# Another order for the hand-over from the expert layer to the last layer of an attention, soft-MoE and SoLU kernel

## The chip, the core and the metric

The kernel runs on one NeuronCore of a Trainium2 chip. The metric is the time of one launch in device microseconds (us), taken as the median of repeated runs. The core has five engines that work through queues of their own: TensorE (PE in the profile; its weight loads are PEld), VectorE (DVE), ScalarE (ACT), GpSimd (POOL) and SyncE (SP, which issues DMAs). An engine runs its instructions strictly in the order in which the program gives them, and waits on semaphores where it needs what another engine makes. So one waiting instruction also holds up what stands behind it on its engine.

## The reference

Three layers follow each other. The last one reads what the middle one writes for all 3072 tokens.

```python
def _attn_ref(q, k, v, mem_k, mem_v):            # 4 batches, 8 heads, 768 tokens, 64 wide, chunks of 32
    ...                                          # softmax(q k / 8) v over a window and 8 memory keys
def _moe_ref(x, phi, w1, w2):                    # x: 3072 x 512, 8 experts of 4 slots, F = 1024
    logits = x @ phi
    d = np.exp(logits - logits.max(0, keepdims=True))
    d /= d.sum(0, keepdims=True) + 1e-09
    slot_input = (d.T @ x).reshape(E, S_per_e, D)
    for e in range(E):
        slot_out[e] = np.maximum(slot_input[e] @ w1[e], 0.0) @ w2[e]
    c = np.exp(logits - logits.max(1, keepdims=True))
    c /= c.sum(1, keepdims=True) + 1e-09
    return c @ slot_out                          # 3072 x 512
def _moe2_ref(x, w_in, w_out, g_ln):
    h = x @ w_in                                 # 3072 x 1024
    e = np.exp(h - np.max(h, axis=-1, keepdims=True))
    solu = h * (e / (np.sum(e, axis=-1, keepdims=True) + 1e-09))
    mu = np.mean(solu, axis=-1, keepdims=True)
    var = np.mean((solu - mu) ** 2, axis=-1, keepdims=True)
    return ((solu - mu) / np.sqrt(var + 1e-06) * g_ln) @ w_out
```

## The kernel before

**Stages.** Until about 115 us the kernel does attention and the dispatch sums of the experts; until 168.8 us the experts' matmuls, while their weights still come in; then a hand-over of some 20 us; then the last layer over 24 tiles of 128 tokens, to the end. The change touches the hand-over and the first tiles of the last layer.

**The hand-over.** Since `h = (c @ slot_out) @ w_in = c @ M` with `M = slot_out @ w_in`, the kernel makes M once (32 rows, 1024 columns) and then each tile's `h` (128 x 1024, two PSUM banks) from M and that tile's `c`. `slot_out` lies in bank 4 as four partial sums. `m_so` (L556) copies it to SBUF in two halves, both on ACT, and sums and turns it on PE (L562); DVE copies the result (L563). `m_in` (L566) multiplies by `w_in` in four parts (L569), which ACT copies out (L573, L574) as `mps`. Tile 0 takes its `h` straight from `mps` in plain fp32, in two halves (`emit_h(0)`, L662). The other tiles wait for M in a rounded form: `m_sum` (L581) sums M on PE, one half into the PSUM bank that later takes tile 0's output and one half into tile 1's `h`; `m_top` (L584, ACT) rounds it, `m_low` (L588, DVE) takes what was rounded off. Their `h` is then two fast matmuls (L662 again, from `m4`). `keep_clock` (L550) issues matmuls whose results nobody reads.

**A tile of the last layer.** DVE takes the maximum of `h` (`emit_max`, L668); ACT the exponential `e` and its sum (`emit_e`, L671); DVE the product `u` of both and its sum (`emit_u`, L677), which ends the use of `h`; `emit_y` (L689 to L697) takes the mean off and rearranges. There are two buffers of `h` (`h0`, `h1`), so tile n+2's `h` may not be written before tile n's `u` is done. For tiles 0 to 3 PE turns `y` (eight transposes, L719), ACT rounds the result (`emit_hi`, L740) and DVE takes the rest (`emit_lo`, L744); for tiles 4 to 23 the turn goes through DRAM and a DVE transpose (L733). Then come 24 matmuls of 128x512 (`emit_main`, L750): eight of hi by the rounded weights `whi`, eight of hi by their low parts `wlo`, eight of lo by `whi`. ACT scales the output by `rstd` (L768), which GpSimd works out (L704 to L716). `sq` (L700) is ACT's sum for the variance.

**The last weights.** `whi` and `wlo` of `w_out`'s last eighth (`wh7`) are made during the hand-over: seven steps of `wout_ops` (L632), each an `l` in `TAIL`: ACT L604 and L605, DVE L608 to L622, ACT L639 for `whi`, DVE L643 for `wlo`. PE needs them for the last matmuls of tile 0.

**What sets the order.** The engines' order is the order of the calls. In the hand-over it is the list `TAIL` (L57). From there on `final` (L778) gives each step of each tile a due time and calls them in the order of these times: `begin` (when a tile's matmuls should start) and `front` (when its front part should) come from a few numbers and the table `FRONT` (L52) for the first tiles, `HS` (L53) holds the times of the first tiles' `h`, and `OFF` (L55) holds the offsets of a tile's steps. The times only sort; what an engine really waits for is a semaphore.

Of the kernel before, what the change touches and what calls it, by code (L numbers as in the profile page):

```python
# [7 lines left out]
FP32 = mybir.dt.float32  # L8
# [25 lines left out]
FC = FF // P  # L34
# [14 lines left out]
NCONST = 425  # L49
NPE, NZ = 4, 4  # L50
T0, TPE, TDM, TF, LEAD, TT, TO, TH = 6.2, 6.85, 5.51, 3.0, 16.3, 3.8, 6.3, 2.2
FRONT = (0.0, 5.5, 8.1, 15.5, 15.1)  # L52
HS = (0.0, 1.2999999999999998, 4.8, 10.3, 12.9)  # L53
YON = 'daddp'
OFF = {'max': 0.25, 'e': 1.7, 'u': 3.3, 'y': 3.6, 'sq': 5.25, 'var': 5.75, 'rstd': 10.0, 'yt': -2.6, 'hi': -2.1, 'lo': -0.1, 'st': 3.65, 'fe': 7.75, 'tr': 0.0, 'hi2': 0.45, 'lo2': 3.95, 'mh': 0.68, 'ml0': 3.4, 'ml': 0.21, 'l0': 0.7, 'l1': 7.25}  # L55

TAIL = (  # L57
    "so open l l l min l l e12 ha hb max s0 s1 t0 e keep w0 u t1 y0 y1 l w1 yt0 hi0 yt1 hi1 lo0 l lo1 e3"
).split()

SPR = ("pp", "ap")
# [3 lines left out]
CLATE = 3  # L65
TORD = [1, 0]
TKEEP = [2, 1]
KEEP = (0, 2, 0, 10)

KS = GREC * REC  # L70
KT = GREC * CH
# [7 lines left out]
def tile_kernel(ctx: ExitStack, tc: tile.TileContext, kr, vr, w1, w2, w_in, w_out, cst, out):  # L79
# [45 lines left out]
    def bank(i):  # L125
        return banks[i]
# [428 lines left out]

    def m_so():  # L556
        for half in range(2):
            act.copy(out=so_sb[:, 256 * half:256 * half + 256], in_=bank(4)[:, 256 * half:256 * half + 256])
        bk = bank(2)
        keep_clock(bank(5), KEEP[1])  # L560
        for k in range(KC):
            pe.matmul(out=bk[:, k * 32:(k + 1) * 32], lhsT=so_sb[:, k * 128:(k + 1) * 128], rhs=i4, start=True, stop=True)  # L562
        dve.tensor_copy(out=sot, in_=bk[:, 0:128].rearrange("p (k s) -> p k s", k=KC))  # L563
        keep_clock(bank(5), KEEP[2])

# [13 lines left out]
    def m_sum(half):  # L579
        sl = slice(512 * half, 512 * half + 512)  # L580
        pe.matmul(out=m_of(half), lhsT=i4rep, rhs=mps[:, sl], start=True, stop=True)  # L581
# [50 lines left out]
    def wout_ops(j, t):  # L632

        w = wo[t % len(wo)]

        def hi():
            area(f"w{j}", [(f"wh{j}", DM), (f"wl{j}", DM)])
            whi[j], wlo[j] = at(f"wh{j}", 0, DM, FP32R), at(f"wl{j}", 0, DM, FP32R)
            act.activation(out=whi[j], in_=w, func=ACTF.Copy, scale=g_sb[:, j:j + 1])  # L639

        return cast_ops(slot_of["wout", j], at("tmp", 512 * (t % 2), 512), w, dve) + [
            hi,
            lambda: dve.scalar_tensor_tensor(  # L643
                out=wlo[j], in0=w, scalar=g_sb[:, j:j + 1], in1=whi[j].bitcast(FP32), op0=ALU.mult, op1=ALU.subtract
            ),
        ]


    def tps(i, sl):
# [2 lines left out]
        return fin["t"][:, sl]  # L652

    def sc(name, i):
        k = ("nm", "s", "nu", "vs", "x", "t", "r").index(name)
        o = 64 + 16 * (i % 8) + k
        return small[:, o:o + 1]

# [7 lines left out]

    def emit_max(i):
        dve.tensor_reduce(out=sc("nm", i), in_=fin["h"][i % 2], axis=AX.X, op=ALU.max, negate=True)  # L668

    def emit_e(i):  # L670
        act.activation(  # L671
# [106 lines left out]
    def final():  # L778

        steps = []  # L780

        def put(t, f, *args):
            steps.append((t, len(steps), f, args))

        begin = [T0]
        for n in range(NTILE):
            begin.append(begin[-1] + (TPE if n + 1 < NPE else TDM))
        front = list(FRONT)
        for n in range(len(front), NTILE):
            front.append(max(front[-1] + TF, begin[n] - LEAD))  # L790
        for n in range(NTILE):
            a, b = front[n], begin[n]
            w = OFF
            if n >= 1:
                put(HS[n] if n < len(HS) else a - TH, emit_h, n)
                put(a + w["max"], emit_max, n)
                put(a + w["e"], emit_e, n)
                put(a + w["u"], emit_u, n)
                put(a + w["y"], emit_y, n)
            put(a + w["sq"], emit_sq, n)  # L800
            put(a + w["var"], emit_var, n)
            put(a + w["rstd"], emit_rstd, n)
            if 1 <= n < NPE:
                for f in range(FC):
                    put(b + w["yt"], emit_yt, n, f)
                put(b + w["hi"], emit_hi, n)
                put(b + w["lo"], emit_lo, n)
            if n >= NPE:
                put(a + w["st"], emit_store, n)
                put(a + w["fe"], emit_fetch, n)  # L810
                put(b - TT + w["tr"], emit_turned, n)
                put(b - TT + w["hi2"], emit_hi, n)
                put(b - TT + w["lo2"], emit_lo, n)
            if n == NTILE - 1:
                put(b + w["l0"], emit_last, n, 0)
                put(b + w["l1"], emit_last, n, 1)
                continue
            for f in range(FC):
                put(b + w["mh"] * f, main_hi, n, f)
                put(b + w["ml0"] + w["ml"] * f, main_lo, n, f)  # L820
            put(b + TO, emit_out, n)
        for t, _, f, args in sorted(steps, key=lambda x: x[:2]):
            f(*args)

    with tc.manual_schedule():
# [176 lines left out]
        for x in TAIL[:first]:  # L1002
# [3 lines left out]
        ob = [at("ob", 512 * i, 512) for i in range(3)]  # L1006
        sq = at("sq", 0, 1024)
        calls.update(
            h0=lambda: emit_h(0), ha=lambda: emit_h(0, (0,)), hb=lambda: emit_h(0, (1,)), max=lambda: emit_max(0), s0=lambda: m_sum(0), s1=lambda: m_sum(1),
            keep=lambda: keep_clock(fin["o"][1], KEEP[3]), t0=lambda: m_top(0), t1=lambda: m_top(1),  # L1010
            w0=lambda: m_low(0), w1=lambda: m_low(1), e=lambda: emit_e(0), u=lambda: emit_u(0),
            y0=lambda: emit_y(0, 0), y1=lambda: emit_y(0, 1),
# [74 lines left out]
```

## Time and profile before

| | |
|---|---|
| median of 3 runs | 330.57 us (330.4 to 331.27) |
| the profiled execution | 330.6 us, of which 328.8 us from its first to its last instruction |
| PE busy | 298.1 us (91%) |
| DVE, ACT, POOL busy | 237.7, 222.3, 168.0 us |
| end of the experts' matmuls | 168.8 us |
| first of tile 0's 24 matmuls | 180.83 us |
| tile 0's last matmul ends | 188.96 us |

Times in the profile are us from the first instruction. An engine's busy time does not tell what holds the kernel up; for this the chain of waits is read, which follows the end of the kernel back to what released each step, and the timeline of an engine, in which the idle time before an instruction and its releaser stand in brackets.

### The profile page before, as it was taken

The page shows a single profiled execution, that of the slowest core. Times are in us where ns is not written, and L with a number is a line of the kernel's source. Part 1 is how long each engine was busy: PE and PEld are TensorE (multiplying, and loading weights), DVE is VectorE, ACT ScalarE, POOL GpSimd, SP SyncE. Part 2 cuts the span into 40 slices and gives each one's busy share as a digit, 9 for nine tenths or more (in the row PEclk, how much of TensorE's full clock was granted, in tenths as well). Part 3 has the DMA queues.
Part 4 walks back from the last instruction along what each step waited for, and adds up shares of the span by engine and source line. Part 5 has one row for each costly group of instructions (what it writes and reads, how often), then busy time and mean ns, then how long its engine had stood idle before and what let it go on. Part 6 is the DMA issues. An engine that isn't in the chain of part 4 may idle for free.

```text
span 328.8 us, 8291 instructions
## 1 busy us (share of the span) xinstructions
PE 298.1 (91%) x3069; PEld 217.1 (66%) x3069; DVE 237.7 (72%) x431; ACT 222.3 (68%) x441; POOL 168.0 (51%) x395
## 2 busy tenths in 40 slices
PE   2788898899797789888999999999999999999996
PEld 2576666777675433323335788888888888888885
DVE  6676887798778439999127986878878878787540
ACT  3566745866774537685536689998888888888721
POOL 5256577676675023233100557777676576676700
PEclk9999999999999999999999999999999999999999
DMA  7999999999999999999930005675756666566521
GB/s 290 420 380 400 418 413 418 416 412 401 415 421 420 419 425 426 424 425 421 421 141 0 1 35 218 232 251 205 244 219 204 252 207 223 220 235 234 194 96 65
DMA packets 32696, 95.85 MB, mean 291 GB/s; under 512 B 3856, under 2 KB 14480, under 8 KB 28944
## 3 DMA queue, kind: packets, MB, share of 16 engines
q1 hardware_dynamic: 32512, 95.11, 74.1%
q8 instruction: 24, 0.39, 0.5%
q10 hardware_dynamic: 144, 0.22, 0.2%
q14 instruction: 16, 0.13, 0.1%
HBM read 78.53 MB, written 16.78 MB: 290 GB/s over the span
## 4 chain that ended last, share of the span: by engine, by line
PE 63%; DMA 17%; DVE 10%; issue 3%; POOL 3%; ACT 2%; SPq 1%; POOLq 0%; ACTq 0%; DVEq 0%
PE bank L750 37%; DMA kq_area<-in_kr_dram 8%; PE bank L281 5%; DMA ex_area<-in_w_dram 5%; PE bank L337 4%; DMA e_area<-in_w_dram 4%; PE h L662 4%; POOL kq_area L330 3%; PE bank L319 2%; PE bank L360 1%; PE bank L407 1%; PE bank L348 1%; PE bank L524 1%; PE bank L760 1%; PE t L760 1%
## 5 line engine op out<-in xcount | busy, mean ns | idle before, releaser
L750 PE MATMUL bank<-wh_area,yh_area 128*128 128x512 f32 x552 | 129.8, 390 | 0.0
L750 PEld LDWEIGHTS bank<-wh_area,yh_area 128*128 128x128 f32 x552 | 103.4, 188 | 21.8
L330 POOL TENSOR_SCALAR kq_area<-kq_area 64x416 f32<-64x416 f32 x88 | 38.4, 441 | 36.5 <-DMA kq_area<-in_kr_dram 17.6
L281 PE MATMUL bank<-kq_area 128*32 128x128 f32 x768 | 29.7, 290 | 15.2 <-POOL kq_area L330 8.2
L733 DVE STREAM_TRANSPOSE yq_area<-yq_area 128x1024 f32<-128x1024 f32 x20 | 24.9, 1245 | 18.7 <-DMA yq_area<-z 18.7
L322 ACT COPY s_area<-bank 128x384 f32<-128x384 f32 x32 | 15.3, 478 | 33.3 <-PE bank L319 31.7
L677 DVE SCALAR_TENSOR_TENSOR eb_area<-h,eb_area 128x1024 f32<-128x1024 f32 x24 | 29.1, 1216 | 8.3 <-ACT eb_area L671 7.9
L281 PEld LDWEIGHTS bank<-kq_area 128*32 128x32 f32 x768 | 20.7, 115 | 21.5 <-POOL kq_area L330 12.1
L299 DVE TENSOR_REDUCE cst_area<-bank 128x6 f32<-128x384 f32 x32 | 17.7, 554 | 18.3 <-PE bank L281 18.0
L337 PE MATMUL bank<-vz_area,s_area 128*32 128x130 f32 x768 | 28.4, 275 | 2.7 <-DVE cst_area L299 1.2
L668 DVE TENSOR_REDUCE cst_area<-h 128x1 f32<-128x1024 f32 x24 | 29.0, 1216 | 0.9 <-PE h L662 0.9
L715 POOL TENSOR_SCALAR cst_area<-cst_area 128x1 f32<-128x1 f32 x72 | 25.4, 353 | 7.6
L671 ACT ACTIVATE eb_area<-h,cst_area 128x1024 f32<-128x1024 f32 x24 | 26.7, 1111 | 1.9 <-DVE cst_area L668 1.9
L700 ACT ACTIVATE eb_area<-eb_area,cst_area 128x1024 f32<-128x1024 f32 x24 | 27.3, 1138 | 0.1
L697 ACT ACTIVATE eb_area<-eb_area,cst_area 128x1024 f32<-128x1024 f32 x20 | 23.1, 1154 | 4.6 <-DVE eb_area L677 4.1
L744 DVE TENSOR_TENSOR yh_area<-yq_area,yh_area 128x1024 fp32r<-128x1024 f32 x20 | 24.5, 1226 | 2.3 <-ACT yh_area L740 2.3
L704 POOL TENSOR_SCALAR cst_area<-cst_area 128x1 f32<-128x1 f32 x24 | 15.6, 648 | 20.6 <-ACT eb_area L671 18.7
L740 ACT CAST yh_area<-yq_area 128x1024 fp32r<-128x1024 f32 x20 | 21.0, 1050 | 6.8 <-DVE yq_area L733 6.7
L716 POOL TENSOR_SCALAR cst_area<-cst_area 128x1 f32<-128x1 f32 x72 | 22.0, 305 | 7.1
L337 PEld LDWEIGHTS bank<-vz_area,s_area 128*32 128x32 f32 x768 | 21.7, 109 | 5.1 <-ACT s_area L355 1.4
L768 ACT ACTIVATE eb_area<-bank,cst_area 128x512 f32<-128x512 f32 x23 | 15.8, 686 | 8.5 <-POOL cst_area L706 5.5
L314 ACT ACTIVATE s_area<-s_area 128x384 f32<-128x384 f32 x32 | 17.0, 530 | 3.3 <-DVE s_area L305 3.2
(154 smaller groups left out, 526.5 us busy)
## 6 DMA issues: line engine op xcount, KB each, us to landing
e_area<-in_w_dram SPq DMA_DIRECT2D x15, 1024.0 KB, 9.9
kq_area<-in_kr_dram SPq DMA_DIRECT2D x32, 400.0 KB, 7.5
vz_area<-in_vr_dram SPq DMA_DIRECT2D x32, 390.0 KB, 6.8
ex_area<-in_w_dram SPq DMA_DIRECT2D x10, 1024.0 KB, 13.4
z<-eb_area SPq DMA_DIRECT2D x20, 512.0 KB, 2.7
yq_area<-z SPq DMA_DIRECT2D x80, 128.0 KB, 2.9
out_dram<-eb_area SPq DMA_DIRECT2D x23, 256.0 KB, 2.0
e_area<-in_w_in_dram SPq DMA_DIRECT2D x4, 1024.0 KB, 9.4
```

What stands on the lines that cost most here:

```text
L281: pe.matmul(out=bk[32 * j:32 * j + 32, t * 128:(t + 1) * 128], lhsT=kq[i][:, KT + c * CH:KT + (c + 1) * CH], rhs=kwin(g % 2, c), start=Tru ...
L330: pool.tensor_scalar(out=o, in0=i, scalar1=1.0, scalar2=0.0, op0=ALU.mult, op1=ALU.add)
L337: pe.matmul(out=bk[32 * j:32 * j + 32, t * 2 * VW:(t + 1) * 2 * VW], lhsT=atb[g % 2][:, c * CH:(c + 1) * CH], rhs=vz[g // 2 % 2][:, :, g % ...
L668: dve.tensor_reduce(out=sc("nm", i), in_=fin["h"][i % 2], axis=AX.X, op=ALU.max, negate=True)
L671: act.activation(out=eb[i % FIN], in_=fin["h"][i % 2], func=ACTF.Exp, bias=sc("nm", i), accum_out=sc("s", i))
L677: dve.scalar_tensor_tensor(out=ub[i % FIN], in0=fin["h"][i % 2], scalar=-1.0 / FF, in1=eb[i % FIN], op0=ALU.mult, op1=ALU.mult, accum_out= ...
L697: act.activation(out=yb[i % FIN], in_=ub[i % FIN], func=ACTF.Identity, scale=-float(FF), bias=sc("nu", i))
L700: act.activation(out=sq, in_=ub[i % FIN], func=ACTF.Square, scale=-float(FF), bias=sc("nu", i), accum_out=sc("vs", i))
L715: pool.tensor_scalar(out=t, in0=r, scalar1=r, scalar2=xx, op0=ALU.mult, op1=ALU.mult)
L733: dve.transpose(out=yv[i % FIN].rearrange("p (f a t) -> p a f t", f=FC, a=4), in_=yq[i % FIN].rearrange("p (a f t) -> p a f t", f=FC, a=4),)
L744: dve.tensor_tensor(out=yl[i % FIN][:, sl], in0=tps(i, sl) if i < NPE else yv[i % FIN], in1=yh[i % FIN][:, sl].bitcast(FP32), op=ALU.subtract,
L750: pe.matmul(out=fin["o"][i % 2], lhsT=a[i % FIN][:, f * 128:(f + 1) * 128], rhs=w[f], start=start, stop=stop)
```

## The change

It has six parts, all between 168.8 us and the first four tiles. (1) The second half of the slots' sum is copied by DVE instead of ACT. (2) Tile 0's maximum is taken by halves: each half of `h` is followed by its own reduction, and a small DVE instruction joins the two. (3) On ACT tile 0's exponential comes ahead of the two roundings of M, and on DVE `u` and the first half of `y` ahead of the two low parts of M. (4) The `h` of tiles 1 to 3 and their maxima move: tile 1's `h` and maximum stand in `TAIL` behind tile 0's first two main matmuls, tile 2's `h` two matmuls later, and the fronts of tiles 2 and 3 and the `h` of tiles 4 and 5 get later due times. (5) The low part of the last weights goes to GpSimd in two instructions. (6) Eight instead of ten `keep_clock` matmuls stand in the hand-over.

```diff
-FRONT = (0.0, 5.5, 8.1, 15.5, 15.1)
-HS = (0.0, 1.2999999999999998, 4.8, 10.3, 12.9)
+FRONT = (0.0, 5.5, 9.7, 16.6, 15.1, 22.0)
+HS = (0.0, 0.0, 6.9, 10.3, 15.0, 21.9)
...
-    "so open l l l min l l e12 ha hb max s0 s1 t0 e keep w0 u t1 y0 y1 l w1 yt0 hi0 yt1 hi1 lo0 l lo1 e3"
+    "so open l l l min l l e12 ha ma hb mb l l s0 s1 e t0 keep u t1 y0 y1 w0 w1 yt0 hi0 yt1 hi1 lo0 f0 h1 x1 lo1 e3"
...
-KEEP = (0, 2, 0, 10)
+KEEP = (0, 2, 0, 8)
...
-            act.copy(out=so_sb[:, 256 * half:256 * half + 256], in_=bank(4)[:, 256 * half:256 * half + 256])
+            move("ad"[half], so_sb[:, 256 * half:256 * half + 256], bank(4)[:, 256 * half:256 * half + 256])
...
-            lambda: dve.scalar_tensor_tensor(
+            lambda: low(w, j) if j == FC - 1 else dve.scalar_tensor_tensor(
                 out=wlo[j], in0=w, scalar=g_sb[:, j:j + 1], in1=whi[j].bitcast(FP32), op0=ALU.mult, op1=ALU.subtract
             ),
         ]
+
+    def low(w, j):
+        pool.tensor_scalar(out=w, in0=w, scalar1=g_sb[:, j:j + 1], scalar2=0.0, op0=ALU.mult, op1=ALU.add)
+        pool.tensor_tensor(out=wlo[j], in0=w, in1=whi[j].bitcast(FP32), op=ALU.subtract)
...
+    def max_half(half):
+        dve.tensor_reduce(
+            out=sc("nm1" if half else "nm", 0), in_=fin["h"][0][:, part(half)], axis=AX.X, op=ALU.max, negate=True
+        )
+        if half:
+            dve.tensor_tensor(out=sc("nm", 0), in0=sc("nm", 0), in1=sc("nm1", 0), op=ALU.min)
...
-            if n >= 1:
+            if n >= 2:
                 put(HS[n] if n < len(HS) else a - TH, emit_h, n)
                 put(a + w["max"], emit_max, n)
+            if n >= 1:
                 put(a + w["e"], emit_e, n)
...
-                put(b + w["mh"] * f, main_hi, n, f)
+                if n or f:
+                    put(b + w["mh"] * f, main_hi, n, f)
```

In the changed file the lines stand lower: L662 became L666, L671 L682, L677 L688, L700 L711, L719 L730, L740 L751, L750 L761, L768 L779; L675 and L679 are `max_half`, L649 and L650 `low`. `Activation`, `DVE` and `Pool` are the semaphores of these engines.

**TensorE around tile 0's `h`.** `h_2249` is `h0`, `h_2250` is `h1`, `bank_84` and `bank_85` are the two output banks. Before:

```order
L569 MATMUL bank_85<-cst_area 32x512 x4
L662 MATMUL h_2249<-hr_area 128x512 [waits Activation_49] x2
L581 MATMUL bank_84<-hr_area,cst_area 128x512
L581 MATMUL h_2250<-hr_area,cst_area 128x512
L550 MATMUL bank_85<-wh_area,c4t_area 128x512 x10
```

Now:

```order
L569 MATMUL bank_85<-cst_area 32x512 x4
L666 MATMUL h_2249<-hr_area 128x512 [waits Activation_49]
L666 MATMUL h_2249<-hr_area 128x512 [waits DVE_49,Activation_49]
L581 MATMUL bank_84<-hr_area,cst_area 128x512
L581 MATMUL h_2250<-hr_area,cst_area 128x512
L550 MATMUL bank_85<-wh_area,c4t_area 128x512 x8
```

The second half of `h0` now also waits for DVE: for the first half's reduction (L675), the last DVE instruction that the program puts ahead of it.

**TensorE from tile 0's transposed `y` of the next tile to tile 1's matmuls.** `t` is the bank pair of the transposes. Before:

```order
L719 MATMUL t<-cst_area,eb_area 128x128 x7
L750 MATMUL bank_84<-wh_area,yh_area 128x512 x5
L662 MATMUL h_2249<-m_area,c4t_area 128x512 [waits DVE_49]
L662 MATMUL h_2249<-m_area,c4t_area 128x512
L750 MATMUL bank_85<-wh_area,yh_area 128x512 [waits Activation_49]
L750 MATMUL bank_85<-wh_area,yh_area 128x512 x9
```

Now:

```order
L730 MATMUL t<-cst_area,eb_area 128x128 x7
L761 MATMUL bank_84<-wh_area,yh_area 128x512 x3
L761 MATMUL bank_84<-wh_area,yh_area 128x512 [waits Pool_49]
L761 MATMUL bank_84<-wh_area,yh_area 128x512
L761 MATMUL bank_85<-wh_area,yh_area 128x512 [waits Activation_49]
L761 MATMUL bank_85<-wh_area,yh_area 128x512 x5
L666 MATMUL h_2249<-m_area,c4t_area 128x512 [waits DVE_49]
L666 MATMUL h_2249<-m_area,c4t_area 128x512
L761 MATMUL bank_85<-wh_area,yh_area 128x512 x13
```

Tile 4's `h` (in `h0`) moved from ahead of tile 1's matmuls to behind the sixth of them; the same pattern stands one tile later with tile 5's `h` in `h1`. From tile 6's `h` on, both orders are alike.

**ScalarE from tile 1's exponential on.** Before:

```order
L671 ACTIVATE eb_area,cst_area<-h_2250,cst_area 128x1024 [waits DVE_49]
L671 ACTIVATE eb_area,cst_area<-h_2249,cst_area 128x1024 [waits DVE_49,Activation_49]
L700 ACTIVATE eb_area,cst_area<-eb_area,cst_area 128x1024 [waits DVE_49]
L740 CAST yh_area<-t 128x1024 [waits PE_49]
L768 ACTIVATE eb_area<-bank_84,cst_area 128x512 [waits PE_49,Pool_49]
```

Now:

```order
L682 ACTIVATE eb_area,cst_area<-h_2250,cst_area 128x1024 [waits DVE_49]
L711 ACTIVATE eb_area,cst_area<-eb_area,cst_area 128x1024 [waits DVE_49]
L751 CAST yh_area<-t 128x1024 [waits PE_49]
L682 ACTIVATE eb_area,cst_area<-h_2249,cst_area 128x1024 [waits DVE_49]
L779 ACTIVATE eb_area<-bank_84,cst_area 128x512 [waits PE_49,Pool_49]
```

Tile 2's exponential (from `h_2249`) moved from right behind tile 1's to behind tile 1's rounding (the CAST), which waits for PE's transposes.

## Rows read from the trace of the kernel before

**Rows 1.** The page, busy time by engine and the granted clock in 40 slices

```profile
PE 298.1 (91%) x3069; PEld 217.1 (66%) x3069; DVE 237.7 (72%) x431; ACT 222.3 (68%) x441; POOL 168.0 (51%) x395
...
PEclk9999999999999999999999999999999999999999
```

**Rows 2.** Stretches: length, busy PE, PEld, DVE, ACT, POOL, clock, DMA share, GB/s

```profile
86.80:88.40 1.60, 0.13 (x5) 0.07 (x8) 1.31 (x4) 1.60 (x7) 1.39 (x4) 1.00 0.98 395
187.50:325.70 138.20, 138.15 (x640) 115.04 (x638) 101.98 (x109) 109.59 (x154) 86.27 (x252) 1.00 0.56 197
```

**Rows 3.** Chain of waits through the hand-over: start, us, what

```profile
172.62 1.93 PE h L662 x4
...
175.91 1.22 ACT eb_area L671 x2
...
177.16 1.25 DVE eb_area L677 x2
...
184.63 1.24 DVE eb_area L677 x2
...
188.96 0.46 PE h L662 x2
```

**Rows 4.** Timeline of ACT and PE, 168.5 to 172.6: start, us, idle before

```profile
168.81 0.65 ACT L558 COPY cst_area<-bank 128x256 f32<-128x256 f32 x2 [2.95 <-PE bank L542]
...
169.26 1.05 PE L562 MATMUL bank<-cst_area 128*128 128x32 f32 x8
```

**Rows 5.** Groups: count, then busy us and mean ns of one

```profile
L299 DVE TENSOR_REDUCE cst_area<-bank 128x6 f32<-128x384 f32 x32 | 17.7, 554 | 18.3 <-PE bank L281 18.0
...
L330 POOL TENSOR_SCALAR kq_area<-kq_area 64x416 f32<-64x416 f32 x44 | 25.0, 568 | 34.6 <-DMA kq_area<-in_kr_dram 17.6 <-PE bank L337 6.5 <-ACT kq_area L326 5.0
...
L622 POOL TENSOR_TENSOR cst_area<-cst_area 128x512 f32<-128x512 f32 x8 | 10.4, 1302 | 0.7
...
L693 POOL TENSOR_SCALAR eb_area<-eb_area,cst_area 128x1024 f32<-128x1024 f32 x1 | 1.1, 1127 | 0.1
...
L413 DVE COPY cst_area<-bank 96x512 f32<-96x512 f32 x1 | 0.7, 687 | 0.3 <-PE bank L407 0.3
...
L563 DVE COPY cst_area<-bank 128x128 f32<-128x128 f32 x1 | 0.3, 291 | 4.7 <-PE bank L562 4.7
```

**Rows 6.** Timeline of DVE

```profile
172.99 0.69 DVE L622 TENSOR_TENSOR wo_area<-wo_area,cst_area 128x512 f32<-128x512 f32 x1
174.57 1.22 DVE L668 TENSOR_REDUCE cst_area<-h 128x1 f32<-128x1024 f32 x1 [0.89 <-PE h L662]
...
178.83 0.74 DVE L588 SCALAR_TENSOR_TENSOR m_area<-cst_area,h 128x512 fp32r<-128x512 f32 x1
...
182.15 2.35 DVE L668 TENSOR_REDUCE cst_area<-h 128x1 f32<-128x1024 f32 x2
...
186.57 1.22 DVE L677 SCALAR_TENSOR_TENSOR eb_area<-h,eb_area 128x1024 f32<-128x1024 f32 x1
...
188.89 1.23 DVE L744 TENSOR_TENSOR yh_area<-t,yh_area 128x1024 fp32r<-128x1024 f32 x1 [0.30 <-ACT yh_area L740]
```

**Rows 7.** Timeline of DVE and POOL around 97.5: a small SBUF instruction beside GpSimd

```profile
97.28 1.29 POOL L622 TENSOR_TENSOR cst_area<-cst_area 128x512 f32<-128x512 f32 x1
...
97.57 1.02 DVE L375 TENSOR_TENSOR cst_area<-cst_area 96x1 f32<-96x1 f32 x1
```

**Rows 8.** Timeline of ACT

```profile
179.05 0.71 ACT L639 ACTIVATE wh_area<-wo_area,cst_area 128x512 fp32r<-128x512 f32 x1
179.67 0.58 ACT L740 CAST yh_area<-bank 128x512 fp32r<-128x512 f32 x1
...
187.84 1.02 ACT L740 CAST yh_area<-t 128x1024 fp32r<-128x1024 f32 x1 [0.70 <-PE t L719]
```

**Rows 9.** Timeline of PE

```profile
180.83 4.29 PE L750 MATMUL bank<-wh_area,yh_area 128*128 128x512 f32 x18
185.92 0.73 PE L662 MATMUL h<-m_area,c4t_area 128*128 128x512 f32 x2 [0.81 <-DVE eb_area L677]
```

## What the change is predicted to do

> **What bounds the kernel now.** I read the page first: TensorE is busy for 298.1 of 328.8 us, no other engine for more than 237.7, and the granted clock is in the top tenth of all 40 slices [rows 1]. Then the stretches. From 187.5 us to the end PE works 138.15 of 138.20 us, at clock 1.00 [rows 2], and its 640 matmuls take 138.15 / 640 = 0.216 us each. So nothing behind 187.5 has any room: a stall that is put into this part costs its full length, and one taken out before it is worth what tile 0's last matmul, which ends at 188.96 [rows 3], moves forward. The chain of waits shows what sets that time: from 172.62 on PE makes tile 0's `h`, then ACT its exponential, DVE `u`, and, some steps later, tile 1's `u`, whose end at 184.63 + 1.24 = 185.87 lets PE start tile 3's `h` [rows 3, 9]. The reader is to see there that PE has no work for 0.81 us before 185.92 [rows 9]. These 0.81 us, and the hand-over ahead of 180.83, are all that the change could win.
>
> **The change part by part.** Times are us in the profiled execution; sizes that the trace lacks are worked out from the nearest rows.
>
> *Copies of the slots' sum.* On ACT the two take 0.65 together, from 168.81 to 169.46 [rows 4]. In the changed order DVE's copy waits for ACT's. For 256 columns from PSUM DVE should need 0.42, between 0.291 for 128 and 0.687 for 512 [rows 5]: about 168.81 + 0.40 + 0.42 = 169.63. PE asks for the second half after half of its eight products, 169.26 + 0.52 = 169.78 [rows 4]. Gain 0; bounds +0.2 (a 0.6 us copy) and -0.1. The Trainium skill, page "PSUM — Partial Sum Buffer", section "PSUM bank collisions raise a hardware error", says that two engines at one bank's same partitions must be kept apart; both copies read bank 4, so by it too two engines give no overlap, and the sum would be the same. No row here shows such a pair.
>
> *Maximum by halves.* DVE's last piece of the weights ends at 172.99 + 0.69 = 173.68 [rows 6], so the first half's reduction runs 173.70 to 174.39: 0.69 is my value for 512 columns, between 0.554 for 384 [rows 5] and 1.22 for 1024 [rows 6]. TensorE's second half now waits for this reduction: the order shows DVE's semaphore at that matmul. It is issued at 174.4 and takes half of 1.93 [rows 3] and a restart of 0.1: 175.4. The second reduction ends at 176.1, the small joining instruction at 176.3 (0.16 for one column: the copies' 0.291 for 128 and 0.687 for 512 [rows 5] grow by 1.03 ns a column), and the exponential starts at 176.4, where it started at 175.91 [rows 3]: +0.5. So halves that should overlap follow each other. Behind PE's wait stand M's two sums, which nobody needs early.
>
> *Low part on GpSimd.* ACT's rounding takes 0.71 [rows 8] and now comes as soon as DVE's piece is ready at 173.68: to 174.4. GpSimd's scaling of 512 columns I put at 0.65 (568 ns for 416, 1127 for 1024), its subtraction at 1.30 [rows 5]: to 176.4. TensorE needs the result in its last matmuls of tile 0, near 188.4: hidden by 12 us, so its cost is nothing unless it disturbs a neighbour. One row shows such a disturbance: a DVE instruction on 96 numbers in SBUF took 1.02 us beside GpSimd's subtraction and ended with it, at 98.59 against 98.57 [rows 7]. The joining instruction at 176.1 is of that kind; it would end with GpSimd, near 176.5, and the exponential start at 176.6: +0.7. The Trainium skill, page "SBUF — State Buffer", section "SBUF: two separate sides", says why: the two engines share a port that one holds for a whole instruction. Without this lock the sum would be 0.2 less; the row agrees with the page. Taking the 0.74 us low part off DVE gains nothing itself, since tile 1's maximum, which stood behind it, will wait for `h`.
>
> *Exponential ahead of M's rounding; later `h`.* Tile 0's first rounding of `y` started at 179.67 and took 0.58 [rows 8]; it moves with the exponential and ends at 180.75 to 180.95. PE's first main matmul follows at 180.9 to 181.1, against 180.83 [rows 9]: four matmuls of `h` stood ahead of it and now come later, which wins back most of the delay. But tile 1's `h` now stands behind two main matmuls and lands some 1.15 later than these begin, at 182.05 to 182.25; before, its maximum started at 182.15 [rows 6], held by DVE. From there exponential and `u` take what they took. **Term A**: -0.05 to +0.2, taken as 0.1. The 0.81 idle is filled by matmuls that stood elsewhere; they are not saved.
>
> *First main matmul of tiles 1 and 2.* Before, the 0.46 pair of tile 4's `h` ran between tile 0's end (188.96 [rows 3]) and tile 1's first main matmul, which covered ACT's rounding, 187.84 + 1.02 = 188.86 [rows 8]. Now PE asks at once. A wait costs more than its length: from `u`'s end at 185.87 to the end of the pair, 185.92 + 0.73 = 186.65 [rows 9], are 0.78 for 0.46 of work, 0.32 for the hand-over. So the first main matmul ends at 188.86 + 0.32 + 0.23 = 189.41 instead of 188.96 + 0.23 = 189.19: 0.22 idle, and again for tile 2. **Term B**: 0.44 (bounds 0 and 0.6).
>
> *Tile 4's and 5's `h`.* They use the buffers of tiles 2 and 3, so they wait for these tiles' `u`. Before, tile 2's `u` ended at 186.57 + 1.22 = 187.79 [rows 6], more than 1 us ahead of PE's pair at 188.96 [rows 3]. In the new order tile 2's exponential stands on ACT behind tile 1's rounding, so it starts at 188.86 and ends with its 1.22 [rows 3] at 190.1; DVE's low part runs 188.89 to 190.12 [rows 6]; `u` ends at 190.12 + 1.24 = 191.36. The pair then ends at 191.36 + 0.78 = 192.14. Without the wait it would end five main matmuls and itself behind 189.41: 189.41 + 1.15 + 0.46 = 191.02. Stall 1.12. The same places stand a tile later (tile 2's rounding, tile 3's exponential, tile 5's `h`): 2 x 1.12. **Term C**: 2.24 (bounds 1.6 to 2.6, if ACT or DVE hands over 0.3 sooner or 0.2 later each time). From tile 6's `h` on the two orders are alike. The stores and fetches of tiles 4 and 5 move with PE, so nothing further is late.
>
> *Fewer filler matmuls.* PE stands idle some 0.7 us before tile 0's transposes. In a stretch with PE busy 0.13 of 1.60 us the clock was 1.00 [rows 2]; cost 0.
>
> The sum: 0.1 + 0.44 + 2.24 = 2.78. The profiled execution took 330.6, the median of the runs 330.57, so no correction between them: 330.6 + 2.8 = **333.4 us**.
>
> **The rivals.**
> *The wait at the second half does not bind, and the lock does not hold.* The second half of `h` lies in another bank than the first reduction reads; if PE passes at 173.6, reductions end at 175.1 and the exponential starts near 175.4, 1.04 earlier than in my walk without the lock (+2.7): +1.7, **332.3**. Against it: the wait stands in the order, with a value that only the first reduction gives, and [rows 7] shows the lock.
> *Faster or same: the later stalls are absorbed.* If PE's rows from 187.5 on hide slack, for example matmuls that wait for weights while they count as busy, terms B and C cost nothing, and the start decides: with the front 1.04 earlier, 330.6 + 0.05 - 1.04 = **329.6**; with the front as I have it, 330.7. It decides from the point at which `u` of tile 2 ends before 190.6. Against it: 0.216 us a matmul over 640 leaves no slack, and `u` stands behind an exponential that can't start before 188.8.
> *Only half of the stall.* If the second stall falls into the shadow of the first (PE's delay gives ACT time to catch up), C is 1.12 and the sum 1.7: **332.2**. Against it: ACT's order binds each tile's exponential to PE's transposes of the same tile, so the delay is carried along.
> *Slower still.* With new idle times of 1 us the granted clock could fall for a while. At 1.2 instead of 2.4 GHz each us of PE's work costs one more: one or two us, **335**. Against it is the clock of 1.00 in [rows 2], around emptier PE.
>
> **How the numbers follow.** The forecast has 0.72. First half's wait not binding: 0.07; half of the stall: 0.05; both end above 332. Absorbed stalls: 0.12, most of it within the third of a per cent. Slower still: 0.04. A measurement here can tell about 0.3% (1.0 us) from no change. Absorbed with the early front is at that bound, absorbed with the late front well within: faster 0.05, same 0.09 (0.02 of it from smaller terms than I bound), slower 0.86. The forecast's own range goes from -0.05 + 0 + 1.6 to 0.2 + 0.6 + 2.6, that is 332.2 to 334.0; with the two rivals near 332.2 and a share of the last one the range is 332.0 to 334.4.
>
> **What would show it.** In the profile after: PE's second half of tile 0's `h` released by DVE near 174.4; the first exponential at 176.4 (no lock) or 176.6, the joining instruction 0.2 or 0.4 long; the first main matmul near 181.0; tile 0's last one ending near 189.1; the pair of tile 4's `h` with some 1.1 us idle ahead of it, released by DVE's `u`, and tile 5's likewise; then no idle time to the end. Wrong would be: the pairs without a wait, tile 2's exponential starting before tile 1's rounding ends, or tile 0's end before 188.5.

## The result and the profile after

The changed kernel took 334.58 us in the median (333.57 to 336.46, 8 runs), the kernel before 331.53 (330.4 to 333.21, 8 runs): ratio 1.0092, 95% interval 1.0063 to 1.012. It is slower by about 3 us, where 2.8 was forecast; but the time itself lies above the range of 332.0 to 334.4, since the level from which it was counted, 330.6, was not the level of these runs.

The profiled execution took 333.97 us, its span is 332.2. In the page TensorE has 1.5 us more work time than in [rows 1], and one slice in which its clock is lower:

```profile
PE 299.6 (90%) x3067; PEld 216.8 (65%) x3067; DVE 238.9 (72%) x433; ACT 222.0 (67%) x440; POOL 170.3 (51%) x397
...
PEclk9989999999999999999999999999999999999999
```

That slice is the third, near 20 us, far ahead of the change. So the two profiles have to be laid over each other at a point just ahead of it: ACT's first copy of the slots' sum, 168.81 before [rows 4], 169.45 after. All times "after the copy" below count from there. This is the hand-over after the change, from the timelines of ACT, DVE, POOL and PE (start, us, idle before and its releaser):

```profile
169.45 0.37 ACT L326 COPY cst_area<-bank 128x256 f32<-128x256 f32 x1 [2.96 <-PE bank L542]
...
177.34 1.12 ACT L682 ACTIVATE eb_area<-h,cst_area 128x1024 f32<-128x1024 f32 x1 [2.19 <-DVE cst_area L679]
...
189.56 1.12 ACT L682 ACTIVATE eb_area<-h,cst_area 128x1024 f32<-128x1024 f32 x1
```

```profile
169.85 0.42 DVE L328 COPY cst_area<-bank 128x256 f32<-128x256 f32 x1 [3.62 <-ACT cst_area L326]
...
174.37 0.69 DVE L675 TENSOR_REDUCE cst_area<-h 128x1 f32<-128x512 f32 x1
176.34 0.69 DVE L675 TENSOR_REDUCE cst_area<-h 128x1 f32<-128x512 f32 x1 [1.28 <-PE h L666]
177.06 0.24 DVE L679 TENSOR_TENSOR cst_area<-cst_area 128x1 f32<-128x1 f32 x1
...
190.83 1.22 DVE L688 SCALAR_TENSOR_TENSOR eb_area<-h,eb_area 128x1024 f32<-128x1024 f32 x1
```

```profile
176.02 1.26 POOL L650 TENSOR_TENSOR wh_area<-wo_area,wh_area 128x512 fp32r<-128x512 f32 x1
```

```profile
175.20 1.10 PE L666 MATMUL h<-hr_area 128*128 128x512 f32 x2 [0.88 <-ACT wh_area L639]
...
181.71 0.73 PE L761 MATMUL bank<-wh_area,yh_area 128*128 128x512 f32 x2 [0.24 <-ACT yh_area L751]
...
192.11 0.74 PE L666 MATMUL h<-m_area,c4t_area 128*128 128x512 f32 x2 [0.74 <-DVE eb_area L688]
...
200.23 0.73 PE L666 MATMUL h<-m_area,c4t_area 128*128 128x512 f32 x2 [0.74 <-DVE eb_area L688]
...
325.98 3.04 PE L771 MATMUL bank<-wh_area,yh_area 128*128 128x256 f32 x24
```

The reader is to see three things. PE stands idle for 0.88 us inside tile 0's `h`, before its second half. The page names ACT's L639 (174.43 to 175.15) as the releaser, but in the program that half waits on DVE for the first reduction, which ended at 175.06, and on ACT for a copy that had long been done (L574, to 173.98): two ends that lie 0.1 apart are easily confused. The exponential begins 7.89 after the copy, where it was 175.91 - 168.81 = 7.10 [rows 3, 4]: 0.79 later. And PE is idle for 0.74 us ahead of tile 4's and of tile 5's `h`, each time until DVE's `u` ends; [rows 2] has 0.05 us of idle time in all from 187.5 us on. From the copy to the end of PE's last matmul it is 325.98 + 3.04 - 169.45 = 159.57 us, before 325.65 - 168.81 = 156.84: 2.73 longer. This stretch is called T below. The chain of waits of the changed kernel goes through exactly the step that the prediction added:

```profile
187.71 0.92 PE t L730 x8
188.65 1.02 ACT yh_area L751
189.69 1.23 DVE yh_area L755
190.92 1.15 DVE eb_area L688 x2
192.07 0.04 issue
192.11 0.74 PE h L666 x2
192.85 3.00 PE bank L761 x13
```

Transposes, rounding, low part, `u`, `h`: a chain from PE over ACT and DVE back to PE, in which the exponential (189.56 above) hides beside the low part. Two orders were turned round here at once: on ACT tile 2's exponential now stands behind tile 1's rounding, and on DVE tile 2's `u` behind tile 1's low part, where before it stood ahead of it (186.57 and 188.89 in [rows 6]). The `u` starts as the low part's row ends, and the exponential's last row ended at 190.76, 0.07 ahead of `u`: by these rows either order alone would have held it about as long. Before, the chain ran through here on PE alone:

```profile
187.80 1.15 PE bank L750 x5
188.96 0.46 PE h L662 x2
189.42 4.33 PE bank L750 x19
```

### The profile page after: what moved, and what is told of

It is laid out like the page before. It is cut to its first block, busy times and chain, and to the rows that moved or that the text cites. A ratio compares the mean times of both kernels' runs of the same rounds, so it can differ in the third digit from the quotient of the medians.

```text
span 332.2 us, 8291 instructions
## 1 busy us (share of the span) xinstructions
PE 299.6 (90%) x3067; PEld 216.8 (65%) x3067; DVE 238.9 (72%) x433; ACT 222.0 (67%) x440; POOL 170.3 (51%) x397
## 4 chain that ended last, share of the span: by engine, by line
PE 61%; DMA 20%; DVE 10%; POOL 2%; ACT 2%; issue 2%; SPq 1%; POOLq 0%; ACTq 0%; DVEq 0%
PE bank L761 36%; DMA kq_area<-in_kr_dram 10%; DMA ex_area<-in_w_dram 5%; PE bank L281 4%; PE bank L337 4%; DMA e_area<-in_w_dram 4%; PE h L666 4%; POOL kq_area L330 2%; DMA vz_area<-in_vr_dram 2%; PE bank L319 2%; PE bank L348 1%; PE bank L360 1%; PE bank L407 1%; DVE eb_area L688 1%; DVE wo_area L613 1%
## 5 line engine op out<-in xcount | busy, mean ns | idle before, releaser
L761 PE MATMUL bank<-wh_area,yh_area 128*128 128x512 f32 x552 | 130.8, 391 | 0.2 <-ACT yh_area L751 0.2
L761 PEld LDWEIGHTS bank<-wh_area,yh_area 128*128 128x128 f32 x552 | 103.1, 188 | 22.9 <-ACT yh_area L751 1.2
L688 DVE SCALAR_TENSOR_TENSOR eb_area<-h,eb_area 128x1024 f32<-128x1024 f32 x24 | 29.1, 1214 | 8.8 <-ACT eb_area L682 6.9
L726 POOL TENSOR_SCALAR cst_area<-cst_area 128x1 f32<-128x1 f32 x72 | 27.3, 380 | 7.6
L682 ACT ACTIVATE eb_area<-h,cst_area 128x1024 f32<-128x1024 f32 x24 | 26.6, 1110 | 4.0 <-DVE cst_area L679 2.2
L672 DVE TENSOR_REDUCE cst_area<-h 128x1 f32<-128x1024 f32 x23 | 27.9, 1217 | 1.4 <-PE h L666 1.4
L711 ACT ACTIVATE eb_area<-eb_area,cst_area 128x1024 f32<-128x1024 f32 x24 | 27.4, 1140 | 2.1 <-DVE eb_area L688 2.0
L727 POOL TENSOR_SCALAR cst_area<-cst_area 128x1 f32<-128x1 f32 x72 | 24.1, 334 | 7.1
L751 ACT CAST yh_area<-yq_area 128x1024 fp32r<-128x1024 f32 x20 | 21.0, 1050 | 6.3 <-DVE yq_area L744 6.1
L779 ACT ACTIVATE eb_area<-bank,cst_area 128x512 f32<-128x512 f32 x23 | 15.8, 686 | 9.0 <-POOL cst_area L717 4.8
L319 PE MATMUL bank<-cst_area,s_area 128*128 128x128 f32 x96 | 17.9, 294 | 0.7 <-ACT s_area L314 0.5
```

The lines of the kernel that those rows point to most:

```text
L319: pe.transpose(out=bk[:, t * 128:(t + 1) * 128], in_=sb_[g % 2][:, t * 128:(t + 1) * 128], identity=ident)
L682: act.activation(out=eb[i % FIN], in_=fin["h"][i % 2], func=ACTF.Exp, bias=sc("nm", i), accum_out=sc("s", i))
L688: dve.scalar_tensor_tensor(out=ub[i % FIN], in0=fin["h"][i % 2], scalar=-1.0 / FF, in1=eb[i % FIN], op0=ALU.mult, op1=ALU.mult, accum_out= ...
L711: act.activation(out=sq, in_=ub[i % FIN], func=ACTF.Square, scale=-float(FF), bias=sc("nu", i), accum_out=sc("vs", i))
L726: pool.tensor_scalar(out=t, in0=r, scalar1=r, scalar2=xx, op0=ALU.mult, op1=ALU.mult)
L761: pe.matmul(out=fin["o"][i % 2], lhsT=a[i % FIN][:, f * 128:(f + 1) * 128], rhs=w[f], start=start, stop=stop)
```

## The experiments

One table first. T was read from two rows of each profile, ACT's first copy and PE's last row; the copy's own time shows how far the execution was then. A, which the expectations use, goes on to the last instruction and takes in the last stores (3.1 to 3.2 us behind T, except in e8). The ratio is that of the timed runs to the kernel before, with its interval.

| kernel | copy at | T | T against before | ratio |
|---|---|---|---|---|
| before | 168.81 | 156.84 | | |
| before again (e0) | 168.25 | 156.84 | 0.00 | 1.001 (0.9979 to 1.004) |
| changed | 169.45 | 159.57 | +2.73 | 1.0092 (1.0063 to 1.012) |
| changed again (e0) | 170.61 | 159.59 | +2.75 | 1.0096 (1.0062 to 1.013) |
| e1 tables back | 169.37 | 157.37 | +0.53 | 1.0045 (1.0018 to 1.0072) |
| e2 FRONT back | 168.75 | 157.94 | +1.10 | 1.0005 (0.9984 to 1.0027) |
| e3 tables alone | 171.71 | 159.38 | +2.54 | 1.0096 (1.0059 to 1.0132) |
| e4 whole maximum | 171.57 | 158.79 | +1.95 | 1.0057 (1.0027 to 1.0087) |
| e5 low part on DVE | 168.94 | 159.56 | +2.72 | one run |
| e6 low part alone | 169.09 | 156.19 | -0.65 | 0.9987 (0.9951 to 1.0023) |
| e8 both halves first | 169.45 | 159.03 | +2.19 | one run |
| e9 turn later | 171.00 | 156.16 | -0.68 | 0.9977 (0.9952 to 1.0002) |

**The level: both kernels again, unchanged.**

> The kernel before, once more, for its level. A = the stretch from ACT's first copy of the slots' sum to the last instruction; it was 160.0 us in the kernel before (168.81 to 328.8) and 162.75 in the changed one (169.45 to 332.2). Theory 1: what lies ahead of A varies by itself between executions, by some 0.5 to 2 us, in either kernel; so here A is 160.0 +/- 0.1, while the copy may come anywhere from 168.5 to 171 and the median lies above 330.6, near 331.5. Theory 2: the 0.64 us ahead of the copy were made by the change; then the copy comes here at 168.8 +/- 0.1 and the median is 330.6.

> The changed kernel, once more. Theory 1 (the level ahead of the hand-over varies by itself): A = 162.75 +/- 0.1 us, the copy anywhere from 168.5 to 171, ratio to before 1.0084 (2.78 of 331). Theory 2 (the change itself delays the stage ahead by 0.64): the copy at 169.45 or later, ratio 1.0103.

Before again, then changed again:

```profile
168.25 0.65 ACT L558 COPY cst_area<-bank 128x256 f32<-128x256 f32 x2 [3.23 <-PE bank L542]
...
322.05 3.04 PE L760 MATMUL bank<-wh_area,yh_area 128*128 128x256 f32 x24
```

```profile
170.61 0.37 ACT L326 COPY cst_area<-bank 128x256 f32<-128x256 f32 x1 [3.67 <-PE bank L542]
...
327.16 3.04 PE L771 MATMUL bank<-wh_area,yh_area 128*128 128x256 f32 x24
```

A was 159.95 and 162.79 and T the same to 0.02 us for each kernel, while the copy came at 168.25 and 170.61; before's median in these runs was 332.43 (330.06 to 334.33, 12 runs). For the kernel before theory 2 falls. The copy at 170.61 alone fits both theories; but over all profiles of the table the copies come at 168.75 to 171.57 with the changed hand-over and at 168.25 to 171.71 with the old one, so the change doesn't set them. Theory 1 stands. Where the time ahead of the copy goes is seen in the stretches from 12 to 28 us. Before again, whose copy came at 168.25 (length; busy PE, PEld, DVE, ACT, POOL; clock; DMA share; GB/s):

```profile
12.00:16.00 4.00, 2.23 (x60) 1.67 (x62) 2.21 (x7) 2.09 (x6) 0.81 (x2) 1.00 1.02 411
16.00:24.00 8.00, 7.05 (x174) 5.87 (x171) 5.60 (x16) 5.17 (x13) 4.21 (x10) 1.00 1.03 410
24.00:28.00 4.00, 3.92 (x107) 3.28 (x102) 3.50 (x11) 3.13 (x9) 1.27 (x3) 1.00 1.00 371
```

And e3, with the same instructions up to the copy, which came at 171.71:

```profile
12.00:16.00 4.00, 1.79 (x51) 1.29 (x43) 1.92 (x7) 0.79 (x2) 0.00 (x0) 1.00 1.01 407
16.00:24.00 8.00, 6.34 (x103) 5.12 (x103) 2.42 (x7) 4.13 (x11) 3.69 (x9) 0.57 0.89 356
24.00:28.00 4.00, 4.00 (x100) 3.46 (x100) 3.79 (x11) 2.86 (x7) 2.24 (x6) 1.00 0.64 200
```

After a stretch in which PE was busy 1.79 of 4 us, its clock was 0.57 (mostly 1.2 instead of 2.4 GHz), and it issued 103 matmuls instead of 174 in the next eight; then the loads slowed to 200 GB/s: from 20 to 32 us the queue that issues them (L201) waited up to 4.8 us at a time for PE's matmuls of L319, in before again up to 3.4. Up to the copy the loads keep the DMA engines at a share near 1 (0.99 over the first 168.7 us of the kernel before), so what they lose here can hardly be made up. A clock of 0.79 in the same stretch goes with copies at 169.37 to 171.00 (changed, e1, e9). But PE's busy time ahead doesn't tell these executions apart. e6, whose order up to the copy is that of before, has the same 1.79 us, then a clock of 1.00 and its copy at 169.09:

```profile
12.00:16.00 4.00, 1.79 (x51) 1.30 (x43) 1.93 (x7) 1.71 (x5) 0.74 (x2) 1.00 1.02 414
16.00:24.00 8.00, 7.18 (x174) 6.00 (x178) 5.58 (x16) 5.38 (x14) 4.30 (x11) 1.00 1.03 413
```

And changed again has a clock of 1.00 there, loads at 308 GB/s and its copy at 170.61, so the clock isn't the only cause; what makes the early part differ was not tested.

**Four tiles only**, to see by the times alone where the spread lies.

```diff
-        for n in range(NTILE):
+        for n in range(NPE):
             a, b = front[n], begin[n]
```

> The kernel before with tiles 0 to 3 alone in the last layer; tiles 4 to 23 and their outputs are left out, some 115 us of the 160 us of A. Theory 1 (the level is set ahead of the hand-over, by when the first loads land and the granted clock of the first 40 us): the spread of the times stays at 2.5 to 4.5 us from lowest to highest over a dozen runs, as with the whole kernel (330.06 to 334.33), and the lowest is near 215. Rival (the spread comes from the last layer, in proportion to its length): 1.5 us or less.

Six runs took 213.28 to 216.58 us. The longest stands alone, at the lowest clock of the six (0.984); the other five lie within 1.3 us (213.28 to 214.54), against 2.9 us in 17 runs of the kernel before beside it (330.14 to 333.06). That is what the rival expected (1.5 or less), but five runs are too few to show a spread, so this experiment decides nothing. What speaks for theory 1 are the profiles: T repeats to 0.02 us in both kernels that were profiled twice, while the copies of the table lie 3.5 us apart.

**The tables taken back.**

```diff
-FRONT = (0.0, 5.5, 9.7, 16.6, 15.1, 22.0)
-HS = (0.0, 0.0, 6.9, 10.3, 15.0, 21.9)
+FRONT = (0.0, 5.5, 8.1, 15.5, 15.1)
+HS = (0.0, 0.0, 6.9, 10.3, 12.9)
```

> The changed kernel with FRONT and with HS from tile 4 on as before, so that the exponentials of tiles 2 and 3 stand ahead of the roundings of tiles 1 and 2, and tile 4's h ahead of tile 1's matmuls. Theory 1 (terms B and C of the prediction, stalls of tiles 4's and 5's h): both go, A falls from 162.75 to 160.4 to 160.6, ratio to before 1.001 to 1.002; no idle time on PE behind 190 us. Rival (the start of the last layer is what costs): A stays above 162, ratio 1.007 or more.

A = 160.53, T +0.53, and behind 190 us PE waits no more. The ratio, 1.0045, lies above what was expected (1.001 to 1.002): the copies of its executions aren't known, and a median of 12 runs from a level that wanders by 4 us tells no more. What remains, 0.53, is more than term A in the changed kernel, since tile 2's maximum now stands ahead of tile 1's `u` on DVE again: `u` starts at 185.73, 16.36 after the copy, in the changed kernel 15.99 (185.44). PE has to wait for it ahead of tile 3's `h`; the chain shows it:

```profile
184.69 1.13 DVE cst_area L672
185.82 1.15 DVE eb_area L688 x2
...
187.01 0.73 PE h L666 x2
...
187.97 0.92 PE t L730 x8
```

Tile 1's transposes start 187.97 - 169.37 = 18.60 after the copy, in the changed kernel 18.26: 0.34 of the 0.53 is this wait.

**FRONT's times of tiles 2 and 3 taken back** (maximum, exponential and `u` early, the `h` of tiles 4 and 5 late).

```diff
-FRONT = (0.0, 5.5, 9.7, 16.6, 15.1, 22.0)
+FRONT = (0.0, 5.5, 8.1, 15.5, 15.1, 22.0)
```

> The changed kernel with only FRONT as before for tiles 2 and 3 (their exponentials early), tiles 4's and 5's h still six matmuls later. Theory 1: term C goes, term B stays: A = 160.9 to 161.1, ratio 1.003; PE idle some 0.1 to 0.25 us before the first main matmul of tiles 1 and 2, no wait at tile 4's h. Rival (the place of the h itself costs, whatever the exponential): A near 162.7.

A = 161.15, a little over what was expected; T is 0.57 longer than with both tables back, and that is term B for two tiles. Term C is gone: the chain goes on PE from the main matmuls to tile 4's `h` without a wait.

```profile
188.29 2.76 PE bank L761 x11
191.06 0.46 PE h L666 x2
...
195.36 2.78 PE bank L761 x11
```

The bubbles of term B stand in no bracket: the 11 matmuls (five of one tile, six of the next) take 2.76 and 2.78 instead of 11 x 0.23 = 2.53. Taking FRONT back moves the exponential on ACT and `u` on DVE together, so no run says which of the two held the changed kernel. The ratio, 1.0005, is below the expected 1.003 as that of e1 is above; between these two the times even have the wrong order.

**The tables alone, on the kernel before.**

```diff
-FRONT = (0.0, 5.5, 8.1, 15.5, 15.1)
-HS = (0.0, 1.2999999999999998, 4.8, 10.3, 12.9)
+FRONT = (0.0, 5.5, 9.7, 16.6, 15.1, 22.0)
+HS = (0.0, 1.2999999999999998, 4.8, 10.3, 15.0, 21.9)
```

> The kernel before with only the later times of the changed FRONT and HS for tiles 2 to 5 (exponentials of tiles 2 and 3 behind the roundings, h of tiles 4 and 5 behind six matmuls); the hand-over as before. A is the stretch from ACT's first copy of the slots' sum to the last instruction, 160.0 us before. Theory 1 (terms B and C, 2.2 us together by runs so far, depend on these times alone): A = 162.2 to 162.7, two idle times of PE of 0.7 us ahead of tiles 4's and 5's h. Rival (they arise only with the late start of the changed hand-over): A = 160.0 to 160.8.

A = 162.59, T +2.54, ratio 1.0096. These numbers alone make nearly the whole loss, with both waits in place:

```profile
190.46 3.01 PE L750 MATMUL bank<-wh_area,yh_area 128*128 128x512 f32 x11
194.21 0.73 PE L662 MATMUL h<-m_area,c4t_area 128*128 128x512 f32 x2 [0.74 <-DVE eb_area L677]
...
202.30 0.73 PE L662 MATMUL h<-m_area,c4t_area 128*128 128x512 f32 x2 [0.74 <-DVE eb_area L677]
```

**The maximum whole again.**

```diff
-... ha ma hb mb l l s0 ...
+... ha hb max l l s0 ...
```

> The changed kernel with tile 0's maximum taken whole again. Theory 1 (the halves run one after the other because PE waits, and cost the hand-over 0.8 us): PE's 0.88 idle inside tile 0's h goes, the exponential starts 0.75 to 0.85 earlier after the copy, and A falls from 162.77 to 161.8 to 162.0. Rival (the exponential is held by something else, GpSimd's subtraction or M's sums): A stays at 162.5 or more.

A = 161.93, T 0.78 less than in the changed kernel. The exponential starts 7.04 after the copy, 0.85 earlier, and 0.06 earlier than before the change: that small step is what it gains from standing ahead of M's rounding.

```profile
177.35 1.23 DVE L672 TENSOR_REDUCE cst_area<-h 128x1 f32<-128x1024 f32 x1 [0.89 <-PE h L666]
```

```profile
178.61 1.12 ACT L682 ACTIVATE eb_area<-h,cst_area 128x1024 f32<-128x1024 f32 x1 [1.33 <-DVE cst_area L672]
```

**Both halves ahead of the first reduction.**

```diff
-... ha ma hb mb l l s0 s1 e t0 keep u t1 y0 y1 w0 w1 yt0 ...
+... ha hb ma mb s0 s1 e t0 keep u t1 y0 y1 w0 w1 l l yt0 ...
```

> The changed kernel with both halves of tile 0's h issued ahead of the first reduction, and the last weights' steps behind M's low parts. Theory 1 (PE's wait goes, but both reductions now wait for the second half, since the tile is tracked as one): no idle time on PE inside h; the first reduction starts together with h's end, 0.89 after DVE's piece, both and the joining instruction take 1.55 instead of 1.23, so the exponential starts 0.3 to 0.4 later than with a whole maximum and 0.45 earlier than in the changed kernel; A = 162.0 to 162.4. Rival (only PE's wait was in the way; the halves overlap then): the first reduction starts right behind DVE's piece, the exponential 1.1 to 1.2 earlier than in the changed kernel, A = 161.6 or less.

Now DVE waits as long as for the whole, and the reductions and the joining instruction follow:

```profile
175.23 1.29 DVE L675 TENSOR_REDUCE cst_area<-h 128x1 f32<-128x512 f32 x2 [0.89 <-PE h L666]
176.55 0.16 DVE L679 TENSOR_TENSOR cst_area<-cst_area 128x1 f32<-128x1 f32 x1
```

The first reduction reads the first half alone, and yet it starts with the end of PE's second: the program's wait there is for the tile, that is for both halves, not for the half that is read. The exponential starts 7.34 after the copy: 0.30 later than with one reduction, 0.55 earlier than in the changed kernel; T falls by 0.54. (A is 163.25, over the expected 162.4, because the last stores ended 1 us later than elsewhere in this one execution; T leaves them out.) So halves gain in neither order. Halves in tiles of their own, which could overlap, were not tried.

**The low part on DVE again.**

```diff
-            lambda: low(w, j) if j == FC - 1 else dve.scalar_tensor_tensor(
+            lambda: dve.scalar_tensor_tensor(
```

> The changed kernel with the last low part on DVE in one instruction again, as before. Theory 1 (the joining instruction ends with GpSimd's subtraction, so it is held): it takes 0.15 to 0.17 instead of 0.24 and A falls by 0.05 to 0.1, to 162.7. Rival (0.24 is its own length): it takes 0.24 again, A = 162.77.

The joining instruction took 0.16, and tile 0's transposes came 0.08 earlier after the copy; at the end 0.01 was left of it (A = 162.76). It was lost ahead of tile 1's transposes (18.24 after the copy, against 18.26); the idle time ahead of tile 4's `h` is the same, 0.73 and 0.74. What took the few hundredths isn't shown.

```profile
176.55 0.16 DVE L679 TENSOR_TENSOR cst_area<-cst_area 128x1 f32<-128x1 f32 x1
```

**The low part on GpSimd alone, on the kernel before.**

```diff
-            lambda: dve.scalar_tensor_tensor(
+            lambda: (pool.tensor_scalar(out=w, in0=w, scalar1=g_sb[:, j:j + 1], scalar2=0.0, op0=ALU.mult, op1=ALU.add),
+                     pool.tensor_tensor(out=wlo[j], in0=w, in1=whi[j].bitcast(FP32), op=ALU.subtract)) if j == FC - 1 else dve.scalar_tensor_tensor(
```

> The kernel before with only the last low part on GpSimd, in two instructions. Tile 1's maximum, which stood behind DVE's 0.74 low part, moves up, and so tile 1's u and tile 3's h. Theory 1 (PE's 0.81 idle is the way to the end there): the idle falls to about 0.1, A = 159.2 to 159.5, ratio 0.998, which the times can hardly tell from 1. Rival (DVE is held by GpSimd's use of the shared memory side, or h lands late): A = 159.8 to 160.2.

A = 159.31, T -0.65. Tile 1's maximum starts 12.68 after the copy instead of 13.34, and PE's idle time ahead of tile 3's `h` falls from 0.81 [rows 9] to 185.54 - 185.40 = 0.14:

```profile
181.77 2.35 DVE L668 TENSOR_REDUCE cst_area<-h 128x1 f32<-128x1024 f32 x2
```

```profile
183.65 1.75 PE L750 MATMUL bank<-wh_area,yh_area 128*128 128x512 f32 x7
185.54 0.73 PE L662 MATMUL h<-m_area,c4t_area 128*128 128x512 f32 x2
```

So one of the six parts, put alone, is a gain. The times can't show it: 0.9987 (0.9951 to 1.0023).

**The same, with tile 1's transposes and tile 3's `h` later.**

```diff
-                    put(b + w["yt"], emit_yt, n, f)
-                put(b + w["hi"], emit_hi, n)
+                    put(b + (w["yt"] if n > 1 else -1.95), emit_yt, n, f)
+                put(b + (w["hi"] if n > 1 else -1.949), emit_hi, n)
...
-HS = (0.0, 1.2999999999999998, 4.8, 10.3, 12.9)
+HS = (0.0, 1.3, 4.8, 11.12, 12.9)
```

> The kernel before with the last low part on GpSimd and with the transposes of tile 1 and tile 3's h behind all matmuls of tile 0. Theory 1 (PE then doesn't wait for tile 1's u; what remains is the wait for ACT's rounding ahead of tile 1's first matmul): no idle time ahead of tile 3's h, 0.2 to 0.45 ahead of tile 1's matmuls, A = 159.1 to 159.4, against 159.3 with the low part alone. Rival (the rounding is late by more than its own length): A = 159.8 or more.

A = 159.3, T -0.68: the wait for `u` is gone, and 0.17 us of waiting for the rounding stand in its place. Its ratio is the lowest, 0.9977 (0.9952 to 1.0002), and still not told apart from 1.

```profile
190.65 1.65 PE L750 MATMUL bank<-wh_area,yh_area 128*128 128x512 f32 x6 [0.17 <-ACT yh_area L740]
```

## Why the prediction was right in its steps and wrong in its number

**The step that failed** is the one on the level: "The profiled execution took 330.6, the median of the runs 330.57, so no correction between them". Three runs from 330.4 to 331.27 were taken for the kernel's time. In the 29 runs beside e0 to e2 the same kernel had a median of 331.85 and went from 330.32 to 333.9. To 331.53, the median beside the changed kernel, the forecast sum of 2.78 gives 334.3, inside the range; 330.6 + 2.73, the measured difference of T, gives 333.3, next to the forecast. The range took in the bounds of every term and nothing for the level, whose spread (about 3 us, 330.32 to 333.9) is larger than all of them.

**The sum.** Forecast 2.78, measured 2.73 in T; the ratio gives 0.0092 x 331.53 = 3.05 (2.1 to 4.0). That the sum is off by 0.05 only is luck in part: its terms A, B and C were off by +0.09, +0.13 and -0.27.

**Term A**, forecast 0.1 (up to 0.2): in the chain PE's transposes of tile 1 start at 187.71 - 169.45 = 18.26 after the copy; in that of before they started at 186.88, which is 18.07: 0.19. But it is a difference of two larger parts. With the maximum whole (e4) these transposes start 17.47 after the copy (189.04 - 171.57): the halves cost 0.79, and the rest of the new hand-over wins 0.60. Which of its parts wins that, no run separates. The low part's move isn't it: the prediction put its removal from DVE at nothing "since tile 1's maximum, which stood behind it, will wait for `h`", and in the changed kernel that holds (e5: 0.01); where `h` stands early it gains 0.65 (e6).

**Halves and lock.** Both reductions and the wait of PE came as forecast (exponential 0.79 later, forecast 0.7). PE's second half ended 0.26 later than forecast, though (176.30 - 0.64 = 175.66, since the two copies lie 0.64 apart; forecast 175.4), and the lock cost less. The joining instruction took 0.24 beside GpSimd's subtraction and 0.16 without it (e5); it ended at 177.30, the subtraction at 177.28. The price was 0.08, not the 0.2 set for it, since the joining instruction began only 0.22 ahead of the subtraction's end. The Trainium skill, page "SBUF — State Buffer", section "SBUF: two separate sides", has the loser wait for the whole of the other's instruction. That the two end together fits a lock; but the instruction's own 0.16 did not come on top of the wait, and here the measurement decides (GpSimd's ends in a trace are rough). The GpSimd instruction of [rows 7], which the prediction calls a subtraction, is an addition of the same shape (L622).

**Term B**, forecast 0.44, was 0.57 (e2 against e1). **Term C**, forecast 2.24, was 2.54 - 0.57 = 1.97: e3 holds both on an unchanged hand-over. (The changed kernel is 1.63 longer than e2: there the old FRONT costs the 0.34 of e1.) Each stall is 0.74 of idle time and 0.28 by which the pair takes longer than 0.46, 1.02 instead of 1.12; the exponential was as late as forecast, but PE, held up longer by term B, asked some 0.06 later, and `u` started 0.09 before the low part's row ended.

**The copies, the filler** cost nothing, as forecast: the sum's copy on DVE (L563) came 1.55 after ACT's first copy, before 1.54, and the clock in the hand-over stayed at 1.00.

**The rivals.** Absorbed stalls fell with e3, half of the stall with the two equal waits of 0.74, the first half's wait not binding with the 0.88 idle. A lower clock did show, but at 20 us and with either hand-over (changed, e1 and e4; e3 and e9).

## What to carry to other kernels

Where an engine is busy without a gap to the end, order decides: an instruction put behind a wait on one engine (here tile 2's exponential behind a rounding on ACT, and its `u` behind a low part on DVE) comes back as a wait on another, here PE. Compare two profiles from a point just ahead of the change; here the stretch behind it repeats to 0.02 us while whole runs differ by 1%. And take a kernel's level, and its spread, from many runs before a difference is added to it.

## What was not expected of the hardware

A clock of 0.57 from 16 to 24 us, in two of the thirteen profiles (e3 and e4), goes with a hand-over that begins at 171.7 and 171.6 instead of 168.3 to 169.5 in most, though over these 168 us the share of the DMA engines is 0.99, near its full; that the clock is the cause isn't shown. And a reduction of 512 columns from PSUM took 0.69 us, of 1024 columns 1.22 to 1.23. Two halves apart add up to 0.16 more than one whole; one right behind the other (e8) they took 1.29, 0.06 more, besides what joins them.
